# Retention and two expert layers on one core: the second experts' second product by seven sub-products, in passes 2 and 3

## The chip, the cores and the metric

One core of a Trainium2 chip. The metric is the device time of one execution in microseconds, as the median of several runs. TensorE (PE), VectorE (DVE), ScalarE (ACT), GpSimd (POOL) and SyncE (SP, which only issues transfers here) work through queues of their own, each in its order, and wait for one another by semaphores.

## The reference

Three stages, one after the other. `x` has 2304 tokens and 512 features; an expert layer has 8 experts with 1024 hidden features.

```python
scores = scale * np.matmul(q, k.transpose(0, 1, 3, 2))          # 4 batches, 8 heads, 576 positions, 64
attn = np.matmul(scores * Dmat, v)                              # Dmat: decay with distance, causal

for e in range(E):                                              # first experts: each token goes to one
    h = np.maximum(x[expert_idx == e] @ w1[e], 0.0)
    out[expert_idx == e] = gate_w[expert_idx == e, None] * (h @ w2[e])

for e in range(E):                                              # second experts: each token goes to all
    h = np.maximum(x @ w1[e], 0.0)
    out += P[:, e:e + 1] * (h @ w2[e])                          # P: 8 rounds of row and column scaling
```

## The kernel before

Every float32 operand of a large product is split into two terms, a rounded one (`hi`) and the rest (`lo`), and each product is three matmuls: hi x hi, hi x lo, lo x hi. ScalarE makes `hi` by a copy, VectorE or GpSimd `lo` by a subtraction (`lo_of`, L215).

The second experts take nearly all of the time after 378 us. They go over the tokens in 3 passes (`NP`) of 768, in each over the 8 experts, and for each expert over four units of 128 + 128 hidden features. A pass's tokens are two halves of 384 (`GRP`). A unit (`unit`, L1149) holds:

- the first product by Winograd's scheme, seven products in place of eight: `product(j, ...)` is 6 matmuls with 128x128 weights as stationary operand and 384 tokens as moving columns (L1163 to L1165). They add up in two PSUM banks, `xb` and `yb`, so that the bank has to be copied (`keep`, L1144, ScalarE) or summed (`h_sum`, L1132, VectorE) before the next product is added to it;
- the second product of the unit before (`second`, L1086): for each of 6 token tiles 2 x 3 matmuls with hidden features as stationary operand and 512 output features as columns (L1096 to L1098). It adds up over the four units in six banks and is taken out once an expert and tile (`finish`, L1102, L1114 on VectorE), with the weight P; after the last expert rows are scattered to the output (L100).

The order is written out by hand: blocks of 9 matmuls of `second` stand between two products of the first. The weights stream: raw parts of 512 KB arrive in `raw_p` (L211, on SP), and `split_step` (L218) makes slots of a ring of four, some steps ahead; for first weights GpSimd first makes the sums and differences that the scheme needs (L251, L252), for each pass anew. The operands of the next pass are loaded (`xload`), summed (`xsums`, GpSimd) and split (`xsplit`) in the last units of a pass (`renew`). `clock`, `tick` and `arrives` are estimates that decide only where in the order a split is put.

Of the kernel before, what the change touches and what calls it, by code (L numbers as in the profile page):

```python
# [18 lines left out]
# columns of the packed constants (they depend on the shapes alone)  # L19
C_KS, C_ID, C_LT, C_BASE, C_EXP, C_CAP, NCONST = 0, 40, 168, 296, 305, 313, 321  # L20
# Tokens that the units of the first experts take: the first unit has the expert with the most tokens
# once PICK_AT tiles of 128 are routed, the others follow by their numbers of tokens. Where an expert has
# more than its unit takes, all of them go by anyhow() instead.
# batches, positions and features of a head
SHAPE = (4, 576, 64)
CAPS = (384, 352, 328, 320, 304, 296, 288, 280)
PICK_AT = 10
# [8 lines left out]
def kernel(  # L36
# [33 lines left out]
    ring_p = ctx.enter_context(tc.tile_pool(name="ring", bufs=4))  # L70
# [4 lines left out]
    # what the first experts give, [feature, token], the tokens' rows and logits, one expert after the other  # L75
    x2 = dram.tile([DM, 2 * N], F32, name="x2")
    rid = dram.tile([2 * N, 1], I32, name="rid")
    lg2d = dram.tile([2 * N, E], F32, name="lg2d")

# [15 lines left out]
    def scatter(key, dst, idx, src):  # L95
        """Rows of src to distinct rows of dst: no two scatters of one key meet in a row."""
        if scatters.get(key):
            # no two scatters follow each other directly, so that none has to wait for the one before
            nc.gpsimd.memset(gap, 0.0)
# [7 lines left out]
    # ------------------------------------------------------------ constants  # L107
# [9 lines left out]
    # of the units: experts, places in the list, first outputs, tiles of 128, whether any exceeds its unit,  # L117
    # and first outputs whatever exceeds
    tab = const.tile([128, 6, E], I32, name="tab")

    # ------------------------------------------------------------ weight stream
    # Weights arrive as raw parts of 512 KiB and are split into two float32r terms in slots of a
    # ring, four steps to a slot, some slots ahead of the products that take them.
# [57 lines left out]
    for p in range(NP):  # L181
# [9 lines left out]
    # An estimate of when, by the tensor engine's clock, what has been issued so far is there: so that  # L191
    # no engine is made to wait for a load while it has other work.
# [86 lines left out]
    # ------------------------------------------------------------ attention  # L279
    tiles = _tiles()  # L280

    work = ctx.enter_context(tc.tile_pool(name="work", bufs=1))
    # the operands of products whose other operand are weights: tokens, then hidden features
# [9 lines left out]
    with ExitStack() as at:  # L293
# [5 lines left out]
        # decay and mask of [key, query] within a tile, of even and of odd heads  # L299
# [17 lines left out]
        def warm(n):  # L317
            """Products of ones while the first loads are under way: the tensor engine's clock rises with use"""
            p = bank(7)
            for _ in range(n):  # L320
                nc.tensor.matmul(p[:, 0:128], onesb, onesb, start=True, stop=True)
# [27 lines left out]
        def scale(t):  # L349
            """With the decay from the first position: the queries for the state and the keys that enter it"""  # L350
# [9 lines left out]
        def scores(t):  # L360
            """[key, query] of each head, two heads at a time in the halves of the array"""
# [17 lines left out]
        def states(t):  # L379
            """What the state gives to each head, [feature, query]"""  # L380
# [11 lines left out]
        def new_state(t):  # L392
            """The state after the chunk"""
# [16 lines left out]
        def attend(t):  # L410
            """[feature, query] of each head, two heads at a time"""
# [15 lines left out]
        def xout(t):  # L427
            """Rows of x times their gate, which is positive: it goes through the first expert's relu"""
# [9 lines left out]
            if t < B:  # L438
                # the first gathers, of other rows, find all rows written
# [641 lines left out]
    with ExitStack() as m2:  # L1081
# [67 lines left out]
        def unit(u, pre, mids):  # L1149
# [3 lines left out]
            if u["i"] % 2:  # L1153
                pre["w2"] = u["w2"] = take()
# [216 lines left out]
```

## Time and profile before

| | |
|---|---|
| three runs | 1898.59, 1903.05, 1906.12 us; median 1903.05 |
| profiled execution | span 1900.9 us from the first to the last instruction; of its own time only this span is given |
| attention, routing, first experts | 0 to about 378 us |
| second experts, pass 1 | about 378 to 882 us |
| passes 2 and 3 | about 882 to 1893 us, handover between them near 1383 us |
| TensorE busy | 97% of the span; VectorE 56%, ScalarE 41%, GpSimd 38% |

How to read it: TensorE's busy time is the union of matmul times, and a matmul's time holds the filling and emptying of the array, which overlaps its neighbours; what one costs in a row is the distance between two starts. Idle time of an engine has the work behind it that ended the wait.

### The profile page before, as it was taken

The numbers are of one execution on the slowest core, as the hardware profiler recorded it, in microseconds if no ns is written. First come the engines' busy times: TensorE is split into PE (matmuls) and PEld (weight loads), VectorE is DVE, ScalarE is ACT, GpSimd is POOL, SyncE is SP. The second block draws the span as 40 slices with busy tenths as digits, with TensorE's granted clock in tenths as the row PEclk, the third lists the DMA queues.
The fourth block names the chain that finished last, engine by engine and source line by source line (L and its number), as shares of the span: only waits on it lengthen the run. The fifth ranks groups of instructions, "written<-read, shape, count | busy, mean of one in ns | idle before, by whom it ended". The sixth has DMA issues, their size and how long they took to land.

```text
span 1900.9 us, 28236 instructions
## 1 busy us (share of the span) xinstructions
PE 1847.6 (97%) x10499; PEld 1672.2 (88%) x10499; DVE 1055.0 (56%) x2080; ACT 771.8 (41%) x1630; POOL 724.9 (38%) x862
## 2 busy tenths in 40 slices
PE   7788999999999999999999999999999999999998
PEld 6667999998899999998999999999889999999997
DVE  6864447546655554556555545555575545555553
ACT  2243455544434334434343344434443434343432
POOL 4544567632332332426432323233453333333232
PEclk9989999999999999999999999999999999999999
DMA  9855555531212122222222222232232222121210
GB/s 258 255 144 171 191 192 172 182 103 45 78 56 78 58 87 91 77 67 73 83 78 66 68 67 67 67 101 67 67 100 67 67 67 72 62 78 56 78 44 34
DMA packets 132093, 182.23 MB, mean 96 GB/s; under 512 B 19427, under 2 KB 76003, under 8 KB 131944
## 3 DMA queue, kind: packets, MB, share of 16 engines
q1 hardware_dynamic: 127800, 169.66, 28.4%
q0 software_dynamic: 3712, 9.96, 1.6%
q8 instruction: 85, 1.39, 0.3%
q10 hardware_dynamic: 432, 0.69, 0.1%
q14 instruction: 64, 0.52, 0.1%
HBM read 164.40 MB, written 15.89 MB: 95 GB/s over the span
## 4 chain that ended last, share of the span: by engine, by line
PE 84%; DVE 3%; issue 2%; ACT 1%; POOL 0%; DMA 0%; SPq 0%; POOLq 0%; ACTq 0%; DVEq 0%
PE b L1098 13%; PE b L1096 13%; PE b L1097 13%; PE b L1163 12%; PE b L1165 12%; PE b L1164 12%; PE b L665 3%; PE b L666 3%; PE b L667 3%; DVE lo L215 1%; DVE cl L215 0%; PE b L648 0%; DVE c L1132 0%; DMA rid<-lst 0%; POOL out_dram L100 0%
## 5 line engine op out<-in xcount | busy, mean ns | idle before, releaser
L215 POOL TENSOR_TENSOR lo<-raw,hi 128x256 fp32r<-128x256 f32 x320 | 289.3, 914 | 640.4 <-ACT hi L239 636.4
L1163 PE MATMUL b<-ch,hi 128*128 128x384 f32 x1344 | 454.7, 338 | 6.2 <-DVE c L1132 4.7
L1165 PE MATMUL b<-ch,lo 128*128 128x384 f32 x1344 | 452.9, 337 | 0.0
L1164 PE MATMUL b<-cl,hi 128*128 128x384 f32 x1344 | 452.1, 336 | 0.0
L1098 PE MATMUL b<-hi,HL 128*128 128x512 f32 x1152 | 451.1, 392 | 0.0
L1096 PE MATMUL b<-hi,HH 128*128 128x512 f32 x1152 | 450.7, 391 | 0.0
L1097 PE MATMUL b<-lo,HH 128*128 128x512 f32 x1152 | 450.3, 391 | 0.0
L215 DVE TENSOR_TENSOR lo<-raw,hi 128x256 fp32r<-128x256 f32 (+1 forms) x512 | 304.0, 596 | 153.0 <-ACT hi L239 130.9
L1134 ACT ACTIVATE HH<-c 128x384 fp32r<-128x384 f32 x288 | 151.5, 526 | 530.6 <-DVE c L1132 530.6
L1163 PEld LDWEIGHTS b<-ch,hi 128*128 128x128 f32 x1344 | 253.2, 188 | 29.1 <-DVE c L1132 6.0
L1135 DVE SCALAR_TENSOR_TENSOR HL<-c,HH 128x384 fp32r<-128x384 f32 x288 | 169.2, 588 | 189.3 <-ACT HH L1134 189.3
L1164 PEld LDWEIGHTS b<-cl,hi 128*128 128x128 f32 x1344 | 253.4, 189 | 12.4
L1098 PEld LDWEIGHTS b<-hi,HL 128*128 128x128 f32 x1152 | 216.3, 188 | 46.6
L1165 PEld LDWEIGHTS b<-ch,lo 128*128 128x128 f32 x1344 | 253.3, 188 | 0.0
L1096 PEld LDWEIGHTS b<-hi,HH 128*128 128x128 f32 x1152 | 216.8, 188 | 32.2 <-issue 0.5
L1097 PEld LDWEIGHTS b<-lo,HH 128*128 128x128 f32 x1152 | 216.8, 188 | 32.1
L252 POOL TENSOR_TENSOR sums<-raw 128x256 f32<-128x256 f32 x96 | 73.4, 764 | 392.1 <-DVE lo L215 392.1
L1132 DVE TENSOR_TENSOR c<-b,c 128x384 f32<-128x384 f32 x288 | 158.9, 552 | 91.8 <-PE b L1165 91.6
L239 ACT CAST hi<-raw 128x512 fp32r<-128x512 f32 x320 | 196.1, 617 | 8.5 <-ACTq L786 6.0
L1144 ACT COPY c<-b 128x384 f32<-128x384 f32 x288 | 136.4, 474 | 155.4 <-PE b L1165 155.4
L215 DVE TENSOR_TENSOR lo<-sums,hi 128x512 fp32r<-128x512 f32 x192 | 133.7, 698 | 108.3 <-ACT hi L259 108.2
L1140 DVE SCALAR_TENSOR_TENSOR HL<-b,HH 128x384 fp32r<-128x384 f32 x96 | 53.5, 558 | 192.4 <-ACT HH L1139 192.4
(168 smaller groups left out, 2065.9 us busy)
## 6 DMA issues: line engine op xcount, KB each, us to landing
raw<-in_moe_w_dram SPq DMA_DIRECT2D x256, 512.0 KB, 3.7
kT<-in_kT_dram SPq DMA_DIRECT2D x18, 256.0 KB, 5.9
qT<-in_qT_dram SPq DMA_DIRECT2D x18, 256.0 KB, 4.7
v<-in_v_dram SPq DMA_DIRECT2D x18, 256.0 KB, 5.3
xs<-x SPq DMA_DIRECT2D x18, 256.0 KB, 3.9
x<-x SPq DMA_DIRECT2D x12, 384.0 KB, 5.7
k<-in_k_dram SPq DMA_DIRECT2D x16, 256.0 KB, 5.3
qdec<-in_decays_dram SPq DMA_DIRECT2D x4, 256.0 KB, 6.2
```

The costliest lines, as they stand in the source:

```text
L215: eng.tensor_tensor(lo, x, hi.bitcast(F32), ALU.subtract)
L239: nc.scalar.copy(c.hi[:, o:o + 512], x[:, i:i + 512])
L1096: nc.tensor.matmul(y[t], hh[:, s], w.hi[:, f0:f0 + 512], start=first, stop=False)
L1097: nc.tensor.matmul(y[t], hh[:, s], w.lo[:, f0:f0 + 512], start=False, stop=False)
L1098: nc.tensor.matmul(y[t], hl[:, s], w.hi[:, f0:f0 + 512], start=False, stop=end)
L1132: nc.vector.tensor_tensor(c, ps, add, ALU.add)
L1134: nc.scalar.activation(hh, c, AF.Relu)
L1135: nc.vector.scalar_tensor_tensor(hl, c, 0.0, hh.bitcast(F32), ALU.max, ALU.subtract)
L1144: nc.scalar.copy(c, ps)
L1163: nc.tensor.matmul(ps, a, xh[:, r, :], start=first and r == 0, stop=False, skip_group_check=True)
L1164: nc.tensor.matmul(ps, a, xl[:, r, :], start=False, stop=False, skip_group_check=True)
L1165: nc.tensor.matmul(ps, b, xh[:, r, :], start=False, stop=r == 1, skip_group_check=True)
```

## The change

Pass 1 stays as it is but for one thing: each unit also writes the split sums of its first weights (hi and lo, 14 x 128 columns of 128 rows each, 1.84 MB) to a buffer `w1s` in HBM, from the ring slot, on SP. Ring, slots and units are there for pass 1 alone. After its last unit and the drain of that unit's second product, the ring's memory is given to new pools.

Passes 2 and 3 are 16 steps (an expert in a pass each). The first product is the same 7 x 6 matmuls of 384 columns in each of four quarters; its weights come from `w1s` in four groups a quarter, into five buffers. What it gives is kept as relu(h) in float32 in four quadrants (two halves of tokens by two halves of hidden features, each in two parts `kh`). The second product goes by seven sub-products of the quadrants too: VectorE makes four sums of quadrants for each `kh` in place, GpSimd four sums of the second weights' quadrants, ScalarE and VectorE split all seven operands of either kind (14 weight splits of 512 columns and 14 hidden splits of 768 a step). A sub-product of one `kh` and one tile of 128 tokens is a chunk of 6 matmuls with 256 columns. The sub-products add up in six banks of 256 columns; each has its eviction (21 a step) into one half of an accumulator's row, times P. Chunks of a step stand between the first products of the next step, by `GAPS`; after the last step its 42 chunks run alone.

The order of the other engines is no longer written by hand: each piece of work is a `Task` with an engine, a duration and what it waits for; due times are worked back from TensorE's line, and a list scheduler walks simulated time and issues on each engine the ready task that is due first. The operand sums of pass 3 are VectorE tasks now (GpSimd's before). In the rest only comments are gone.

```diff
+    early = ExitStack()
-    ring_p = ctx.enter_context(tc.tile_pool(name="ring", bufs=4))
+    ring_p = early.enter_context(tc.tile_pool(name="ring", bufs=4))
+    w1s = dram.tile([E * 4, 128, 2, 1792], F32, name="w1s")
...
-    for p in range(NP):
+    for p in range(1):
         for e in range(E):
             for j in range(2):
...
         def unit(u, pre, mids):
             w = take()
+            for k, x in enumerate((w.hi, w.lo)):
+                nc.sync.dma_start(out=w1s[4 * u["e"] + u["i"]][:, k], in_=x[:, 0:1792].bitcast(F32))
+            arrives(5.2)
...
-        n_unit = NP * E * 4
+        n_unit = E * 4
...
+    early.close()
+    with ExitStack() as m3:
+        HB = GRP // 128
+        free = {
+            "w1": slots_of("wa", 5, (128, 2, 512), F32R),
+            "w2": list(zip(slots_of("wbh", 4, (128, 2, 256), F32R), slots_of("wbl", 4, (128, 2, 256), F32R))),
+            "h": slots_of("hq", 14, (128, 2, GRP)),
+            "s": list(zip(slots_of("sh", 3, (128, 2, GRP), F32R), slots_of("sl", 3, (128, 2, GRP), F32R))),
...
+        for s in range(first_s, last_s):
+            p, e = divmod(s, E)
+            for i in range(4):
+                kh = i // 2
...
+                    def wload(_, b=b, c0=c0, c1=c1, n=4 * e + i):
+                        nc.sync.dma_start(out=b.tile[:, :, 0:c1 - c0].bitcast(F32), in_=w1s[n][:, :, c0:c1])
+                    wg[gi].load = Task("SP", 4e-3 * (c1 - c0), wload, takes=b)
...
+                product(0, [prev["x"]])
+                made["p1"] = Task("ACT", 0.37, keeper("p1"), [P_[0]], takes=kb["p1"])
+                product(1, [prev["y"]])
+                a0 = put(0, "DVE", 0.47, adder(0, "p1"), [P_[1], made["p1"]], uses=[kb["p1"]])
+                relu[0, i] = Task("ACT", 0.41, relu_in(0), [a0], uses=[hb[0, kh]])
+                product(2, [made["p1"]])
+                made["u2"] = Task("ACT", 0.37, keeper("u2"), [P_[2]], takes=kb["u2"])
+                product(3, [made["u2"]])
+                made["u3"] = Task("ACT", 0.37, keeper("u3"), [P_[3]], takes=kb["u3"])
+                product(4, [made["u3"]])
+                relu[2, i] = put(2, "ACT", 0.39, relu_ps(2), [P_[4]])
+                product(5, [a0])
+                a3 = put(3, "DVE", 0.47, adder(3, "u3"), [P_[5], made["u3"]], uses=[kb["u3"]])
+                relu[3, i] = Task("ACT", 0.41, relu_in(3), [a3], uses=[hb[3, kh]])
+                product(6, [a3])
+                a1 = put(1, "DVE", 0.47, adder(1, "u2"), [P_[6], made["u2"]], uses=[kb["u2"]])
...
+            UB, US = (0.51, 0.60), (0.73, 0.87)
+            for kh in range(2):
+                t3 = Task("POOL", 1.45, sub(T3[kh], B[1, 1], B[0, 1]), [lb[1, 1], lb[0, 1]], takes=T3[kh], uses=[B[1, 1], B[0, 1]], wide=True)
+                s0 = split("w2", 0, kh, B[0, 0], [lb[0, 0]], UB)
+                t5 = Task("POOL", 1.45, sub(B[0, 1], B[0, 1], B[0, 0]), [t3, lb[0, 0]], uses=[B[0, 1], B[0, 0]], wide=True)
...
+                z4 = Task("DVE", 0.87, add(z4b, Q[1], Q[3]), done[1] + done[3], takes=z4b, uses=[Q[1], Q[3]], wide=True)
+                s0 = split("s", 0, kh, Q[0], done[0], US)
+                z2 = Task("DVE", 0.87, sub(Q[1], Q[0], Q[1]), [z4, *done[0]], uses=[Q[0], Q[1]], wide=True)
+                z0 = Task("DVE", 0.87, sub(Q[0], z4b, Q[0]), [z2, s0], uses=[Q[0], z4b], wide=True)
...
+            def chunk2(j, kh, t, sops=sops, bops=bops, ps2=ps2):
...
+                    for r in range(2):
+                        st = kh == 0 and j in (0, 1, 5) and r == 0
+                        nc.tensor.matmul(ps, hh[:, r, c], wh[:, r], start=st, stop=False, skip_group_check=True)
+                        nc.tensor.matmul(ps, hh[:, r, c], wl[:, r], start=False, stop=False, skip_group_check=True)
+                        nc.tensor.matmul(ps, hl[:, r, c], wh[:, r], start=False, stop=kh == 1 and r == 1, skip_group_check=True)
...
+            for j in range(7):
+                for kh in range(2):
+                    for t in range(HB):
+                        so, bo = sops[j, kh], bops[j, kh]
+                        dep = [so[1], so[2], bo[1], bo[2]]
+                        if kh == 0:
+                            back = {0: 4, 1: 6, 2: 0, 3: 2, 4: 3, 5: 1, 6: 5}[j]
+                            dep.append(ev.get((back, t)) if j > 1 else last_ev.get((back, t)) if s > first_s else None)
+                        c = pe(0.714, chunk2(j, kh, t), dep, uses=[so[0], bo[0]])
+                for t in range(HB):
+                    eng, us, fn = evict(j, t)
...
+        GAPS = (1, 1, 2, 2, 1, 3, 0.5)
+        for s in range(first_s, last_s + 1):
+            b = [g2[s - 1, j, kh, t] for j in range(7) for kh in range(2) for t in range(HB)] if s > first_s else []
+            owed = 0
+            if s < last_s:
+                for i in range(4):
+                    for j in range(7):
+                        line.append(g1[s, i, j])
+                        owed += GAPS[j]
+                        while owed >= 1:
+                            owed -= 1
+                            if b:
+                                line.append(b.pop(0))
+            line += b
```

## Rows read from the trace of the kernel before

**Rows 1.** The page: span, then busy us, share and instructions of an engine.

```profile
span 1900.9 us, 28236 instructions
...
PE 1847.6 (97%) x10499; PEld 1672.2 (88%) x10499; DVE 1055.0 (56%) x2080; ACT 771.8 (41%) x1630; POOL 724.9 (38%) x862
```

**Rows 2.** Stretches: length; busy of PE, PEld, DVE, ACT, POOL; clock; DMA share; GB/s.

```profile
175.00:378.00 203.00, 198.06 (x1400) 191.14 (x1401) 106.34 (x194) 104.19 (x216) 123.42 (x129) 0.98 0.57 182
...
902.00:1362.00 460.00, 460.00 (x2315) 415.79 (x2314) 244.55 (x432) 183.75 (x388) 150.56 (x186) 1.00 0.23 74
1362.00:1402.00 40.00, 37.34 (x178) 33.02 (x177) 28.38 (x37) 18.60 (x35) 26.98 (x25) 0.96 0.22 75
```

**Rows 3.** Groups, whole span: count; busy us, mean ns; idle before, releaser.

```profile
L1163 PE MATMUL b<-ch,hi 128*128 128x384 f32 x1344 | 454.7, 338 | 6.2 <-DVE c L1132 4.7 <-ACT c L1144 0.9
...
L1098 PE MATMUL b<-hi,HL 128*128 128x512 f32 x1152 | 451.1, 392 | 0.0
```

**Rows 4.** TensorE's timeline in a unit of pass 2: start, duration, line, shapes.

```profile
1008.08 0.39 PE L1096 MATMUL b<-hi,HH 128*128 128x512 f32 x1
...
1010.14 0.34 PE L1163 MATMUL b<-ch,hi 128*128 128x384 f32 x1
...
1012.23 0.39 PE L1096 MATMUL b<-hi,HH 128*128 128x512 f32 x1
```

**Rows 5.** TensorE's timeline, the last first experts: first and last of 46.

```profile
371.76 0.29 PE L667 MATMUL b<-HH,lo 128*128 128x280 f32 x1
...
377.52 0.29 PE L667 MATMUL b<-HH,lo 128*128 128x280 f32 x1
```

**Rows 6.** TensorE's timeline in the attention, eight matmuls in one line.

```profile
46.26 1.06 PE L388 MATMUL b<-qs,st 128*128 128x128 f32 x8
```

**Rows 7.** TensorE's timeline at both handovers; brackets: idle before, releaser.

```profile
884.78 0.45 PE L1163 MATMUL b<-ch,hi 128*128 128x384 f32 x1 [2.34 <-DVE c L1132]
...
893.88 0.45 PE L1163 MATMUL b<-ch,hi 128*128 128x384 f32 x1 [0.56 <-ACT c L1144]
...
1385.70 0.69 PE L1163 MATMUL b<-ch,hi 128*128 128x384 f32 x1 [2.33 <-DVE c L1132]
1386.18 0.52 PE L1164 MATMUL b<-cl,hi 128*128 128x384 f32 x1
...
1388.42 0.52 PE L1165 MATMUL b<-ch,lo 128*128 128x384 f32 x1
```

**Rows 8.** The last matmul of a product, and ScalarE's copy of its bank.

```profile
1003.76 0.34 PE L1165 MATMUL b<-ch,lo 128*128 128x384 f32 x1
...
1004.19 0.48 ACT L1144 COPY c<-b 128x384 f32<-128x384 f32 x1 [1.82 <-PE b L1165]
```

**Rows 9.** VectorE's timeline, and below it GpSimd's, in the same unit.

```profile
1008.33 1.16 DVE L215 TENSOR_TENSOR lo<-raw,hi 128x512 fp32r<-128x512 f32 x1
...
1013.13 0.69 DVE L215 TENSOR_TENSOR lo<-sums,hi 128x512 fp32r<-128x512 f32 x1
...
1008.20 0.74 POOL L251 TENSOR_TENSOR sums<-raw,sums 128x256 f32<-128x256 f32 x1
```

**Rows 10.** Groups with shapes kept apart, whole span: count; busy us, mean ns.

```profile
L1132 DVE TENSOR_TENSOR c<-b,c 128x384 f32<-128x384 f32 x288 | 158.9, 552 | 91.8 <-PE b L1165 91.6
...
L1134 ACT ACTIVATE HH<-c 128x384 fp32r<-128x384 f32 x288 | 151.5, 526 | 530.6 <-DVE c L1132 530.6
...
L1114 DVE SCALAR_TENSOR_TENSOR a<-b,P,a 128x512 f32<-128x512 f32 x126 | 86.9, 741 | 2.8 <-PE b L1098 2.8
...
L259 ACT CAST hi<-sums 128x512 fp32r<-128x512 f32 x192 | 118.4, 617 | 6.0 <-POOL sums L251 6.0
...
L358 POOL TENSOR_TENSOR qs<-qT,qdec 128x512 f32<-128x512 f32 x14 | 17.7, 1263 | 1.3 <-PE b L400 0.9 <-DMA qdec<-in_decays_dram 0.4
...
L980 ACT CAST ch<-x 128x768 fp32r<-128x768 f32 x18 | 14.9, 828 | 1.4 <-POOL x L961 1.4
```

**Rows 11.** DMA issues: queue, count, KB each, median us from issue to landing.

```profile
raw<-in_moe_w_dram SPq DMA_DIRECT2D x256, 512.0 KB, 3.7
```

317 lines of the change are left out of this document (316 added, 1 removed).

## Prediction

> **What bounds the kernel now.** I read the page's first part, then the table by stretch, then the groups by line, then TensorE's own timeline. The page says that TensorE is busy for 97% of the span [rows 1]; a share alone doesn't tell whether it works at its peak, so the stretches come next. In the 460 us from 902 to 1362, which lie in passes 2 and 3, TensorE is busy for 460.00 us at granted clock 1.00, VectorE for 245, ScalarE for 184, GpSimd for 151, and the DMA engines for 23% [rows 2]. Nothing else comes near: in these passes the time is the number of matmuls times their spacing. Only around 1362 to 1402, where a pass hands over to the next, does TensorE lose 2.7 us [rows 2].
>
> The mean durations in the groups (338 and 392 ns [rows 3]) are no price, since matmuls overlap. The spacing is: nine matmuls of 512 columns start between 1008.08 and 1010.14, so 2.06 / 9 = 0.2289 us each; twelve of 384 columns take the next 2.09 us, 0.174 each [rows 4]. A unit has 42 of 384 (first product) and 36 of 512 (second product): 7.3 + 8.2 = 15.5 us. An expert has four units in a pass, 62.2 us.
>
> **What the change takes off TensorE.** The first product stays: 168 x 0.174 = 29.2 us for an expert and pass. The second goes from 144 matmuls of 512 columns (144 x 0.2289 = 33.0 us) to 7 sub-products x 2 halves x 3 tiles x 6 = 252 of 256 columns. The columns fall to 7/8, but the number of matmuls rises by three quarters, so all hangs on the spacing at 256 columns, which the trace doesn't have. The nearest row is 280 columns: 45 steps from 371.76 to 377.52 us are 0.128 each [rows 5]. Over columns at 2.4 GHz (0.213, 0.160, 0.117 us) the three rows have 15, 14 and 11 ns more. 256 columns are 0.107 us at that clock; with 11 to 15 ns it is 0.118 to 0.122, and I take 0.119. That is 252 x 0.119 = 30.0 us, 2.97 us less for an expert and pass, and for 16 of them **-47.5 us**. Bounds: -51.5 at 0.118, and -11 us (252 x 0.128 = 32.3 us) if 256 columns are no quicker than 280.
>
> The Trainium skill ("TensorE: Matmul & The Clock Gate", Back-to-back issue gap) gives columns over 2.4 GHz plus 2.5 ns: 215.8 and 109.2 ns, by which the change would take off 57 us; the trace's 0.229 at 512 disagrees, so the rows decide.
>
> **What it adds.**
> The kernel before keeps a block of the second product between any two of the first; the list in the new order keeps one to three chunks there, taken from the expert before. The first expert of pass 2 has no expert before, since the pass-1 loop ends with its own drain. There products 3, 4 and 6 of each quarter stand right behind the copy or sum of the bank that they add to. Such a copy starts 0.26 us after TensorE's next slot (matmul at 1003.76, slot at 1003.93, copy at 1004.19), takes 0.48 [rows 8], so it ends 0.74 us after that slot; the matmul that waited for it then starts, 0.05 later by the estimate from the same pair of engines, and takes 0.45 us where others take 0.34 (893.88 [rows 7]): 0.9 us in all. Twelve of them are **+10.8 us** (8 to 18: the upper end where each also stands behind one 0.62 us cast).
>
> The last expert's second product (30 us) now runs alone at the end, behind its own splits. Of VectorE's work for it, 14 weight residuals at 0.69, 22 operations of 768 columns at 1.04 (0.69 x 768/512) and 21 evictions at 0.45 (between a half of 0.74 and all of it), 42 us [rows 9, 10], about 8 can be done ahead with three split buffers and four weight pairs: 34 against 30, **+4 us** (0 to 12).
>
> In the steady part VectorE has for each expert and pass these 42 us and 12 sums at 0.55, in all 49 us of 59.2 us; ScalarE 12 x 0.47 + 16 x 0.53 + 14 x 0.62 + 14 x 0.83 = 34 us [rows 8, 10]. GpSimd's eight weight sums at about 1.26 us [rows 10] are 10 us, and they can delay VectorE: a 512-column residual alone took 0.69 us, but 1.16 when it started at 1008.33 while a GpSimd sum ran from 1008.20 to 1008.94; from 1008.94 on it is 0.55 to its end [rows 9]. So VectorE waited, it did not share. Full serial cost is 49 + 10 = 59 us, just the period. Orders on all engines are fixed, so a late eviction or copy stops TensorE: queued behind a waiting VectorE sum are evictions of the second product, and the next sub-product of the same bank waits for those. Bounds: 0 (as now) to one late 0.56 us [rows 7] in each quarter, 36 us over all; I take one for each expert and pass, 16 x 0.6 = **+9.6 us**.
>
> The Trainium skill ("SBUF — State Buffer", SBUF: two separate sides) calls that port pair an exclusive lock, held for a whole instruction; the 1.16 us row agrees, and it speaks against this change, which moves VectorE towards its limit.
>
> Handover of pass 2 to 3: now a sum waits 2.33 us at 1385.70 and the nine matmuls after it run 0.32 apart, that is at the lower of the two clocks (1.2 GHz), for another 1.3 us [rows 7]. The new order has the operand sums on VectorE, nine more operations of 1.04 us in about 30 us that have 0 to 10 free for each 59: I keep the same 4 us, **0** (-4 to +6). Handover of pass 1 to 2: the last unit's 2.34 us wait stays, since that code stays; the 0.56 behind it goes, because the drain of 36 matmuls (8.2 us) now stands there: **-1**. The same 8.2 us cover the first loads of pass 2 (512 KB land in 3.7 us [rows 11]) as long as ring slots of earlier units are free; **+1**, 5 without that cover.
>
> Removed at no gain: splits, sums and ring of the first weights in passes 2 and 3, since TensorE doesn't wait for them now [rows 2]. What stands in their place is loads: 4 x 1.84 MB of split weights and 2.1 MB of second weights in 59 us, 160 GB/s; in pass 1 the writes add 32 x 1.84 = 58.7 MB in 32 x 15.5 = 496 us to the 74 GB/s that a pass moves now, 192 GB/s. The stretch 175 to 378 moved 182 GB/s with the DMA engines 57% busy [rows 2], so both fit. The writes stand on SP behind the split of the slot just taken, with the raw loads queued behind them; those run some units ahead: **+1** (0 to 5).
>
> Sum: 1900.9 - 47.5 + 10.8 + 4 + 9.6 + 0 - 1 + 1 + 1 = **1878.8 us** of span. The median of the runs shown is 1903.05, 2.1 above the profiled span; I add that: **1880.9 us**, 1.2% less.
>
> **Rivals.**
> *The weight load becomes the bound.* A multiply of 256 columns is 107 ns; full 128x128 loads with only 128 columns behind them run at (1.06 - 0.29) / 7 = 0.110 us a pair [rows 5, 6] (0.29 for the time of the last one itself, as that of the nearest row), though their columns are half that. So the load needs almost what the multiply does, and if the two don't overlap well, 256 columns stay at the 0.128 of 280. Each ns costs 252 x 16 = 4.0 us: at 0.128, 1917 us, **slower**. It decides from 0.127. Against it: 0.110 is below 0.119, and at 280 columns nothing of it is seen. Chance 9%. The Trainium skill (same page, LDWEIGHTS) prices a load of 128 columns at 107 ns, and the 0.110 row agrees.
>
> *VectorE becomes the pace.* With stops of 2.2 us for each expert and pass it is 1880.9 - 9.6 + 35.2 = 1906 us, no change (12%); from 2.6 us it is slower, 1919 at 3 (6%). For it: the 49 to 59 us against 59. Against: the 59 needs every GpSimd sum to fall on a waiting VectorE operation, and the new order puts two chunks (2 x 6 x 0.119 = 1.4 us) and most often a first product (6 x 0.174 = 1.0 us) between an eviction and the matmul that needs its bank.
>
> *Nothing stops.* No late evictions, handovers covered, a drain in time: 1880.9 - 9.6 - 4 - 4 = 1863 us, faster (20%).
>
> *The reload doesn't do what it says*: weights come late from HBM. One 3.7 us landing exposed for each expert and pass is +59, 1940 us (2%). Against: five buffers, each used some 4 us of 18.
>
> **How the numbers follow.** Forecast 51%, of which 5% lie above the line of no change. What a measurement can tell from no change is 0.5%, 9.5 us: faster is below 1893.5, slower above 1912.5. Faster 0.46 + 0.20 = 0.66; same 0.05 + 0.12 = 0.17; slower 0.09 + 0.06 + 0.02 = 0.17. The range goes from 1855 (nothing stops, 4 less at 0.118 and 4 less at the handover) to 1913, which leaves out the load, slow VectorE and reload cases.
>
> **What would show it.** Spacing of 256-column matmuls in the last 30 us, where nothing else runs: 0.119; 0.127 or more is the first rival. TensorE's idle time by what it waited for: about 11 us in the first 40 us of pass 2, 4 at the end, 10 spread over the rest, on VectorE and ScalarE. VectorE near 50 us of each 59. No wait for loads. Pass 1 unchanged to within 2 us. The forecast falls with the spacing, or with idle time in the middle of a pass above 1.3 us for each expert.

## The result, and the profile after

The changed kernel takes 1880.87 us (median of 4 runs, 1880.26 to 1886.72); the kernel before took 1902.31 us on the same chip (median of 4, 1898.59 to 1906.12). The ratio is 0.9901 with an interval of 0.9879 to 0.9924: 1.0% faster. The profiled execution took 1880.59 us, its span is 1878.8 us. The forecast was 1880.9 us, with a span of 1878.8. That the two agree to the last digit is luck: the mechanism and the largest term were right, but three of the smaller terms were off by 10, 10 and 4 us, one of them because its step was wrong, and they cancel.

The page of the kernel after, against [rows 1] (span; busy us, share and instructions of each engine; then two groups of matmuls with count, busy us, mean ns, and idle time before them by releaser):

```profile
span 1878.8 us, 32676 instructions
...
PE 1803.9 (96%) x12227; PEld 1720.0 (92%) x12227; DVE 1233.2 (66%) x2239; ACT 892.2 (47%) x1718; POOL 575.1 (31%) x599
...
L1566 PE MATMUL b<-wbh,sh 128*128 128x256 f32 x1344 | 379.7, 282 | 2.1 <-DVE ya L1585 2.1
...
L1385 PE MATMUL b<-ch,wa 128*128 128x384 f32 x896 | 304.8, 340 | 17.6 <-ACT kp L1391 7.4
```

The work moved as the change says: GpSimd is busy for 150 us less, VectorE for 178 us more. The last group has what is new: 17.6 us of idle time before the matmuls of the first product, 7.4 of it for one copy, `kp`.

The table by stretch of the kernel after, to be read against [rows 2] (length; busy us of PE, PEld, DVE, ACT, POOL, with instructions; granted clock; DMA share; GB/s):

```profile
376.00:860.00 484.00, 483.74 (x2489) 437.72 (x2488) 267.74 (x508) 197.91 (x417) 158.47 (x191) 1.00 0.54 192
892.00:901.00 9.00, 1.56 (x9) 1.25 (x8) 0.52 (x1) 0.48 (x1) 1.89 (x3) 0.71 1.00 333
901.00:943.00 42.00, 32.98 (x154) 28.78 (x154) 11.23 (x18) 16.87 (x33) 10.26 (x8) 0.90 0.64 197
943.00:1350.00 407.00, 407.00 (x2887) 406.89 (x2886) 308.67 (x465) 223.12 (x399) 69.73 (x53) 1.00 0.54 166
1400.00:1780.00 380.00, 380.00 (x2699) 380.00 (x2698) 285.57 (x430) 207.07 (x371) 77.95 (x65) 1.00 0.54 164
```

Inside a pass TensorE never stops (407.00 of 407 and 380.00 of 380). Most of what is lost lies at one place, 892 to 943, the start of pass 2, in whose first 9 us TensorE worked for 1.56. The traffic is what was forecast: 192 GB/s in pass 1 (192), 166 and 164 in passes 2 and 3 (160).

The spacing, which carries the forecast, in the timeline of TensorE of the kernel after, against [rows 4] (start, duration; first a chunk and a half in pass 2, nine matmuls of 256 columns from 1007.46 up to the 384-column matmul at 1008.54; then the first and the last of the 30 matmuls that end the kernel):

```profile
1007.46 0.28 PE L1566 MATMUL b<-wbh,sh 128*128 128x256 f32 x1
...
1008.54 0.34 PE L1385 MATMUL b<-ch,wa 128*128 128x384 f32 x1
...
1864.48 0.28 PE L1566 MATMUL b<-wbh,sh 128*128 128x256 f32 x1
...
1867.96 0.28 PE L1568 MATMUL b<-wbh,sl 128*128 128x256 f32 x1
```

From 1007.46 to 1008.54 are nine steps, 0.120 each; from 1864.48 to 1867.96 are 29, also 0.120. Over the long stretches 0.1195 fits best. The forecast took 0.119.

**Where the time went.** For the sums below, the "excess" of a stretch is TensorE's time from matmul start to matmul start beyond the plain spacing (0.1195 us at 256 columns, 0.1736 at 384, 0.2285 at 512). From the first matmul of pass 1's units (377.64 before, 377.89 after) to the last matmul of all (1892.61, 1867.96) the kernel takes 1514.97 us before and 1490.07 after: 24.9 less. By terms:

| term | forecast | measured |
|---|---|---|
| 256 columns for 512: 16 x (144 x 0.2285 - 252 x 0.1195) | -47.5 | -44.6 |
| stops of pass 2's first expert behind bank copies and sums | +10.8 | +12.2 |
| handover 1 to 2: the new wait for `kp` 7.6, low clock after it 3.5 | +1 | +11.1 |
| handover 1 to 2: stalls of pass 1's last unit | -1 | -4.6 |
| steady part, 950 to 1350 and 1400 to 1780 (before -0.4, after -1.1) | +9.6 | -0.7 |
| handover 2 to 3 (4.95 before, 1.98 after) | 0 | -3.0 |
| last second product (-0.1 before, 4.5 after) | +4 | +4.6 |
| pass 1, writes (1.93 before, 1.80 after) | +1 | -0.1 |
| sum to the last matmul | -22.1 | -25.1 |
| after the last matmul (8.29 before, 10.84 after) | 0 | +2.55 |
| ahead of pass 1 | 0 | +0.25 |

The terms give -22.3 and the spans differ by -22.1. The stretch 860 to 950, which holds the handover and all twelve stops, has 4.6 us of excess before and 23.3 after.

### The profile page after: what moved, and what is told of

Same layout as the page of the kernel before. It is cut to its first block, busy times and chain, and to the rows that moved or that the text cites. A ratio compares the mean times of both kernels' runs of the same rounds, so it can differ in the third digit from the quotient of the medians.

```text
span 1878.8 us, 32676 instructions
## 1 busy us (share of the span) xinstructions
PE 1803.9 (96%) x12227; PEld 1720.0 (92%) x12227; DVE 1233.2 (66%) x2239; ACT 892.2 (47%) x1718; POOL 575.1 (31%) x599
## 4 chain that ended last, share of the span: by engine, by line
PE 84%; DVE 3%; ACT 1%; issue 1%; DMA 1%; POOL 0%; SPq 0%; ACTq 0%; DVEq 0%; POOLq 0%
PE b L1568 8%; PE b L1567 8%; PE b L1566 8%; PE b L1385 8%; PE b L1386 8%; PE b L1387 8%; PE b L1100 5%; PE b L1102 5%; PE b L1101 5%; PE b L1170 4%; PE b L1172 4%; PE b L1171 4%; PE b L669 3%; PE b L671 3%; PE b L670 3%
## 5 line engine op out<-in xcount | busy, mean ns | idle before, releaser
L1566 PE MATMUL b<-wbh,sh 128*128 128x256 f32 x1344 | 379.7, 282 | 2.1 <-DVE ya L1585 2.1
L1568 PE MATMUL b<-wbh,sl 128*128 128x256 f32 x1344 | 380.3, 283 | 0.5 <-DVE sl L219 0.4
L1567 PE MATMUL b<-wbl,sh 128*128 128x256 f32 x1344 | 380.6, 283 | 0.0
L1385 PE MATMUL b<-ch,wa 128*128 128x384 f32 x896 | 304.8, 340 | 17.6 <-ACT kp L1391 7.4
L1386 PE MATMUL b<-cl,wa 128*128 128x384 f32 x896 | 302.3, 337 | 0.0
L1387 PE MATMUL b<-ch,wa 128*128 128x384 f32 x896 | 300.8, 336 | 0.0
L1568 PEld LDWEIGHTS b<-wbh,sl 128*128 128x128 f32 x1344 | 257.5, 192 | 0.9 <-DVE sl L219 0.9
L1385 PEld LDWEIGHTS b<-ch,wa 128*128 128x128 f32 x896 | 170.6, 190 | 22.7 <-ACT kp L1391 7.8
L1387 PEld LDWEIGHTS b<-ch,wa 128*128 128x128 f32 x896 | 168.9, 189 | 0.0
L1170 PE MATMUL b<-ch,hi 128*128 128x384 f32 x448 | 151.6, 338 | 0.3
L1172 PE MATMUL b<-ch,lo 128*128 128x384 f32 x448 | 150.5, 336 | 0.0
L1171 PE MATMUL b<-cl,hi 128*128 128x384 f32 x448 | 150.3, 336 | 0.0
```

What stands on the lines that cost most here:

```text
L1170: nc.tensor.matmul(ps, a, xh[:, r, :], start=first and r == 0, stop=False, skip_group_check=True)
L1171: nc.tensor.matmul(ps, a, xl[:, r, :], start=False, stop=False, skip_group_check=True)
L1172: nc.tensor.matmul(ps, b, xh[:, r, :], start=False, stop=r == 1, skip_group_check=True)
L1385: nc.tensor.matmul(ps, a, xh[:, r, :], start=first, stop=False, skip_group_check=True)
L1386: nc.tensor.matmul(ps, a, xl_[:, r, :], start=False, stop=False, skip_group_check=True)
L1387: nc.tensor.matmul(ps, b, xh[:, r, :], start=False, stop=r == 1, skip_group_check=True)
```

## The experiments

Each is an edit of the changed kernel. The time before pass 1's units, which no edit touches, differs between the runs (its end lies at 372.81 to 381.19 us), so where a few us matter I count from the first matmul of these units to the last matmul of all: 1490.07 us in the kernel after. Times are medians of four runs unless it says one run; ratios are to the kernel before, run beside them.

**What holds the first copy of pass 2?** The chain of waits of the kernel after, from the last matmul of pass 1 on (start, duration, what), and under it ScalarE's timeline (in brackets the idle time before and what ended it):

```profile
890.76 0.24 PE b L1102
...
891.02 0.76 DVE a L1118
...
891.88 0.96 POOL out_dram L104
...
893.15 6.72 DMA out_dram<-a,idc
...
899.97 0.49 ACT kp L1391
...
900.50 0.69 PE b L1385
```
```profile
899.97 0.48 ACT L1391 COPY kp<-b 128x384 f32<-128x384 f32 x1 [15.23 <-DMA out_dram<-a,idc]
```

The copy of the first bank waits for the transfer of pass 1's last scatter. It is not its data that it needs. The scatter reads an accumulator `a` of pass 1, and the theory is that the memory of `kp`, allocated anew for passes 2 and 3, lies where that accumulator lay. The first edit lets `kp`, `ku`, `kv` take other memory, by allocating them ahead of the split operands:

```diff
+            "p1": slots_of("kp", 1, (128, GRP)),
+            "u2": slots_of("ku", 1, (128, GRP)),
+            "u3": slots_of("kv", 1, (128, GRP)),
             "s": list(zip(slots_of("sh", 3, ...
-            "p1": ...   (the three lines moved up)
```

> The changed kernel with one edit: the three buffers for the bank copies (kp, ku, kv) are laid ahead of the split buffers, so that the first of them no longer lies where pass 1's accumulators were. Theory A (the first copy of pass 2 waits until the last scatter of pass 1 has left the accumulator under it): ScalarE's copy starts some 0.3 us after the first product, the 7.4 us wait of the third product at 900.5 shrinks to about 0.6, TensorE's clock doesn't fall, so the 24 or so matmuls at 0.32 us go back to 0.174: 6.8 + 3.5 = about 10 us less, a span near 1868 us. Rival B (the copy waits for the first weights of pass 2 or for the ring as a whole): the wait stays within 1 us of 7.4, span 1878 to 1880.

1868.15 us (1864.02 to 1870.52), ratio 0.9832 [0.9807, 0.9856]. ScalarE's timeline and TensorE's waits from 885 to 945 us (total us, times, longest):

```profile
890.51 0.48 ACT L1391 COPY kp<-b 128x384 f32<-128x384 f32 x1 [7.38 <-issue]
```
```profile
PE b L1385 <- DVE hq L1397: 2.9, 4, 0.7
PE b L1385 <- ACT ku L1391: 2.4, 4, 0.6
PE b L1385 <- ACT kv L1391: 2.4, 4, 0.6
PE b L1385 <- DMA wa<-w1s: 2.0, 1, 2.0
```

The copy now runs at 890.51 and no longer waits; the 7.4 us wait for `kp` is gone from the list. So it was the memory. Not all comes back: a wait of 2.0 us for the weights, `wa`, shows further on, and the expectation that the clock would not fall failed, since the lower clock follows behind that wait (stretch of this run, under the columns of the table above):

```profile
906.00:912.00 6.00, 5.43 (x18) 4.92 (x16) 1.03 (x1) 0.97 (x2) 4.09 (x4) 0.50 0.80 266
```

That costs some 2.5 us. The excess from 860 to 950 falls from 23.3 to 16.0, and the time between the two matmuls by 8.9 us; of the rest 1.4 us lies in the last second product, where the low clock described below was shorter.

The twelve stops stand there as forecast: three kinds of four, 0.6 to 0.7 us each. In the kernel after one of them is longer, 2.0 us; ScalarE makes that copy behind two casts. Its waits in the same stretch, the two that differ from the list above:

```profile
PE b L1385 <- ACT kp L1391: 7.4, 1, 7.4
PE b L1385 <- ACT ku L1391: 3.8, 4, 2.0
```

The second edit changes the first expert's order so that products 3, 4 and 6 no longer stand right behind the copy or sum of their bank:

```diff
-                    for j in range(7):
+                    for j in (0, 1, 2, 5, 3, 4, 6) if s == first_s else range(7):
```

> The changed kernel with one edit: in the first step of pass 2, where no second product stands between the first products, TensorE takes the seven products of a quarter in the order 0, 1, 2, 5, 3, 4, 6 instead of 0 to 6. Product 5 starts the other bank and so can cover the copy behind product 2, and product 4 the sum that product 6 needs; only the copy behind product 3 stays uncovered. Theory A (what TensorE loses there are three copies or sums of a bank a quarter, 0.9 us each): eight of twelve stops go, some 7 us less, span near 1872 us, with the 7.4 us wait of the first quarter still there. Rival B (the stops are VectorE and ScalarE being behind with the splits of that step, or weights arriving late): the same time is lost at other products, span within 2 us of 1879.

1868.35 us (1863.57 to 1869.16), ratio 0.9834 [0.981, 0.9858]. TensorE's waits from 885 to 945 us:

```profile
PE b L1385 <- ACT kp L1391: 8.0, 1, 8.0
PE b L1385 <- ACT kv L1391: 2.3, 4, 0.6
PE b L1385 <- ACT ku L1391: 0.9, 1, 0.9
```

The copy of `kp` holds it up as before; of the twelve stops the four of `kv` stay and one of `ku`, so seven go where eight were expected. The excess from 860 to 950 is 14.6 instead of 23.3. This is 8.7 us; seven stops at the forecast's 0.9 and 1.1 off the longest one are 7.4, and the lower clock behind the wait for `kp` holds some 1.6 us less, though the wait is 0.6 longer. The profiled span, 1865.9, is 6.1 us below the expected 1872: 2.5 us of that lies again in the last second product and 1.6 ahead of pass 1, neither of which the edit touches.

**How far is VectorE from being the pace?** The forecast allowed 9.6 us for late evictions; none is seen. Either there is much room, or little. Doubling each of GpSimd's weight sums (a second operation on the result, times one) lengthens what GpSimd holds of the port that it shares with VectorE; `sub` and `add` call it:

```diff
+            def again(eng, o, y, z, op):
+                eng.tensor_tensor(o, y, z, op)
+                if eng is nc.gpsimd:
+                    w = o.rearrange("p k (a c) -> p (k a) c", c=128)
+                    eng.tensor_tensor(w, w, ones.unsqueeze(1).to_broadcast([128, 4, 128]), ALU.mult)
```

> The changed kernel with one addition: after each of GpSimd's eight weight sums of a step (passes 2 and 3) GpSimd multiplies the result by ones, another operation of 512 columns with two inputs, so that it works twice as long; the order on every engine stays. Theory A (TensorE is free of VectorE's delays, since VectorE was busy for only 45 of 59 us and two chunks stand behind most evictions): VectorE's busy time goes up by at most 10 us a step, to 55, and TensorE's idle time in the middle of a pass stays under 0.5 us a step: span under 1887 us. Rival B (the forecast's: one late eviction of 0.6 us a step, and more with each collision): 0.6 us or more a step, 16 steps, span 1889 us or more; at a full 1.3 us stop for each added operation far over 1900.

Two more make VectorE's own sum larger: the residuals of the second weights computed twice, and all residuals of the second product computed twice.

```diff
-                    lo_of(nc.vector, o.tile[1], src.tile, o.tile[0])
+                    for _ in range(2 if kind == "w2" else 1):
+                        lo_of(nc.vector, o.tile[1], src.tile, o.tile[0])
```

> The changed kernel with one addition: in passes 2 and 3 VectorE makes the residual of each of the 14 weight splits of a step twice, one right after the other, 8.4 us more a step (14 x 0.6); the order on every engine stays. VectorE goes from 45 to about 54 of 59 us. Theory A (VectorE paces only when its own sum reaches the step, and what doubled GpSimd work cost was its late start of single sums, not its total): at most 0.6 us a step, span under 1889 us. Rival B (the order has so little room that each late operation stops TensorE): 1.5 to 3 us a step as with doubled GpSimd work, whose VectorE was at 48.5 us: span 1903 to 1927 us.

```diff
-                    lo_of(nc.vector, o.tile[1], src.tile, o.tile[0])
+                    for _ in range(2):
+                        lo_of(nc.vector, o.tile[1], src.tile, o.tile[0])
```

> The same for all 28 residuals of a step: 8.4 + 14 x 0.87 = 20.6 us more, VectorE would need 66 us a step. Both theories: it paces. If its sum alone decides, the step is 66 us, 7 more than now, and the span 1879 + 16 x 7 = 1990 us; if waits add to it, more. It gives the point from which VectorE decides.

They took 1923.04, 1952.88 and 2166.33 us (one run each). The stretch 943 to 1350 of each, in this order, under the columns of the table above:

```profile
943.00:1350.00 407.00, 397.02 (x2792) 394.39 (x2791) 334.94 (x448) 212.20 (x384) 153.31 (x100) 1.00 0.53 160
```
```profile
943.00:1350.00 407.00, 391.45 (x2697) 387.87 (x2698) 356.93 (x522) 204.15 (x372) 66.54 (x48) 0.98 0.51 156
```
```profile
943.00:1350.00 407.00, 340.73 (x2228) 329.75 (x2229) 364.89 (x503) 169.26 (x308) 56.96 (x40) 0.96 0.42 129
```

And TensorE's waits in it (total us, times, longest), of the first and of the last:

```profile
PE b L1385 <- DVE hq L1397: 9.5, 8, 1.5
```
```profile
PE b L1385 <- DVE hq L1397: 44.9, 33, 4.1
PE b L1385 <- ACT ku L1391: 14.2, 10, 1.9
PE b L1567 <- DVE ya L1586: 3.5, 4, 0.9
```

An expert and pass is 168 x 0.1736 + 252 x 0.1195 = 59.3 us of plain spacing. The excess of the stretch (-0.5, 12.7, 25.9 and 91.4 us) says how many of these it holds: (407 - excess) / 59.3 = 6.87, 6.65, 6.43 and 5.32. For one expert and pass that makes:

| kernel | VectorE busy | GpSimd busy | excess |
|---|---|---|---|
| after | 44.9 | 10.2 | -0.1 |
| sums on GpSimd twice | 50.4 | 23.1 | 1.9 |
| weight residuals twice | 55.5 | 10.3 | 4.0 |
| all residuals twice | 68.6 | 10.7 | 17.2 |

This is the rival of VectorE's pace, and the runs give its curve. At 44.9 us of 59.3 nothing is lost; at 50.4, with 9 us to spare by its own sum, each expert already loses 1.9 us; at 68.6, 9.3 above the period, it loses 17.2, so 8 us more than the sum. That the gaps would swallow an addition fell with the first of the three, and the numbers for the other two were missed, the last by 175 us of span against VectorE's sum alone. In the first two runs what TensorE waits for is nearly always the sum `hq`. In the first it is one such wait of 1.4 to 1.5 us for each expert and pass, and each time VectorE comes to the sum straight from a weight residual, as here ahead of the matmul at 1020.49, which waited 1.45 us:

```profile
1019.28 0.68 DVE L219 TENSOR_TENSOR wbl<-sums,wbh 128x512 fp32r<-128x512 f32 x1
1019.89 0.55 DVE L1397 TENSOR_TENSOR hq<-b,kv 128x384 f32<-128x384 f32 x1
```

So a sum is late because it stands in a fixed order behind something longer, and TensorE has no slack to win it back. In the third run copies, evictions and residuals are late as well. The first of the three runs shows the price of the shared port too: 12.9 us more of GpSimd lengthened VectorE's busy time by 5.5 us though its instructions are the same (67 in an expert and pass in both). The added time lies in the operations whose two inputs are both in SBUF (a weight residual 711 ns in the kernel after, 950 here); an eviction (478, 476) and a bank sum (555, 550), which read a bank, stay as they were. No engine waited for GpSimd's results in that stretch.

The Trainium skill ("SBUF — State Buffer", SBUF: two separate sides) says that GpSimd and VectorE take that port in turns, one waiting until the other's instruction ends. The 5.5 us are in line with that; how long each wait lasts they don't show.

**How near is the weight load?** A load that needed more than 0.119 us was the rival that ended slower. To see its floor, two of the three matmuls of a triple take 128 columns instead of 256, with the same weight loads (the low terms of the other columns are left out of the result):

```diff
-   nc.tensor.matmul(ps, hh[:, r, c], wl[:, r], ...)
-   nc.tensor.matmul(ps, hl[:, r, c], wh[:, r], ...)
+   nc.tensor.matmul(ps[:, 0:128], hh[:, r, c], wl[:, r, 0:128], ...)
+   nc.tensor.matmul(ps[:, 0:128], hl[:, r, c], wh[:, r, 0:128], ...)
```

> The changed kernel, but in the second product of passes 2 and 3 the two matmuls of each three that carry a low term take only the first 128 of their 256 columns; the low terms of the other columns are left out of the result. Theory A (a matmul's spacing is its columns over the clock and some 12 ns, down to 256 columns and on): 128 columns follow at 0.066 us, a step's second product takes 84 x (0.1195 + 2 x 0.066) = 21 us, the step 50 us, and the span falls by 130 us or more unless VectorE's 45 us a step come into the way. Theory B (the weight load is just under the multiply at 256 columns, by the 0.110 us of the 128-column pairs in the attention): 128 columns follow at 0.110, a step's second product takes 28.5 us instead of 30.1, and the span falls by about 25 us, to 1854. By B the load was not the bound at 256 but lies 9 ns under it.

1876.17 us (one run). The weight loads (PEld) and the matmuls (PE) of one chunk, from the timeline:

```profile
1100.95 0.19 PEld L1568 LDWEIGHTS b<-wbh,sl 128*128 128x128 f32 x1
...
1101.98 0.19 PEld L1568 LDWEIGHTS b<-wbh,sl 128*128 128x128 f32 x1
```
```profile
1100.84 0.28 PE L1566 MATMUL b<-wbh,sh 128*128 128x256 f32 x1
...
1102.83 0.39 PE L1385 MATMUL b<-ch,wa 128*128 128x384 f32 x1
1103.06 0.34 PE L1386 MATMUL b<-cl,wa 128*128 128x384 f32 x1
```

Nine loads take 1.03 us, 0.114 each. The eighteen matmuls take 1.99 us instead of 18 x 0.1195 = 2.15, and the next one is 0.23 instead of 0.17 before its successor, so the chunk is some 0.10 shorter though a third of its columns are gone. From the first matmul of pass 2's second expert to the first of pass 3's last, fourteen experts, it takes 813.3 us instead of 830.8, 1.25 each. By its columns each would have been some 9 us shorter (128 columns at about 0.066, an estimate from columns over 2.4 GHz and the some 12 ns that the wider rows have on top: 168 x 0.053). So a load with its matmul has a floor of 0.114, and 256 columns stand only 5 to 6 ns above it. That the load sets this floor, and not something else that each pair of load and matmul costs, was not tested. The rival was wrong at this width, by a narrow margin, and with a load for each matmul anything narrower has little left to gain: 4032 x 0.0055 = 22 us in the whole kernel.

The Trainium skill ("TensorE: Matmul & The Clock Gate", LDWEIGHTS) gives a load's time as its columns over 1.2, in ns, by which 128 columns would take 107 ns (an estimate from that formula); in this run they come 114 ns apart.

**Both gains together.** The two edits of the handover, and a due time for the last scatters, which had none, so that the evictions ahead of them would be placed earlier:

```diff
+        for t in given.values():
+            t.due = clock_
         for t in reversed(order):
```

> The two edits of the earlier runs together (bank copies' buffers first; order 0, 1, 2, 5, 3, 4, 6 in the first step of pass 2), and the last row scatters are given a due time, so that the evictions before them aren't put off behind everything else. Theory A (the costs were separate): the excess of TensorE's spacing in the first step falls from 23 us to four copies of 0.75 us and some 2 us of weights that come late, about 5 us; the last scatter starts 1 to 2 us sooner after the last matmul (now 4.0 us). Span 1878.8 - 18 - 1.5 = about 1859 us. Rival B (with the stops gone, the first weights from HBM become late): the wait moves to the loads, span 1863 to 1868.

1861.84 us (1859.05 to 1863.45), ratio 0.9797 [0.9775, 0.9818]. TensorE's waits from 885 to 945, the first of its final scatters in GpSimd's timeline, and the same one of the kernel after:

```profile
PE b L1385 <- DMA wa<-w1s: 3.9, 2, 2.2
PE b L1385 <- ACT kv L1391: 2.4, 4, 0.6
```
```profile
1843.95 0.98 POOL L104 DMA_INDIRECT out_dram<-ya,idc  x1 [22.11 <-DVE ya L1585]
```
```profile
1865.65 0.99 POOL L104 DMA_INDIRECT out_dram<-ya,idc  x1 [23.52 <-DVE ya L1585]
```

From the first matmul of pass 1's units to the last it takes 1473.45 us, 16.6 less than after: 15.0 at the first handover (23.3 to 8.3) and 2.7 at the second handover and at the end, with 1.2 lost again in small parts over the passes. The due time did nothing: the first scatter starts 2.31 us ahead of the last matmul (1846.26 here, 1867.96 after) in both kernels. And part of the gain went into a new wait, 3.9 us for the first weights.

Those weights are issued late. The theory of the last run is that they wait for memory of pass 1 as `kp` did, so in the combined version the accumulators and the three copies were allocated ahead of everything else:

```diff
+        acc = slots_of("ya", 3 * HB, (128, DM))
         free = {
+            "p1": ..., "u2": ..., "u3": ...   (moved ahead of the other kinds)
```

> The combined version with the memory laid out once more: the accumulators of passes 2 and 3, which are first written a step later, take the first place of the ring's memory, then the bank copies, then the weight buffers. Theory A (SP's loads were late in the first step because the third weight buffer lay on the ring slot that the drain reads, so that SP stood from 866 to 891 us with all second weights queued behind): the loads are issued before the drain ends, the two waits for first weights of 1.6 and 2.2 us in the first step go, span 1857.3 - 4 = about 1853 us. Rival B (the first step asks more of HBM than it gives, 7.3 MB and second weights in 40 us): the waits move by the time of some loads but stay, span 1856 to 1859.

1858.11 us (1854.01 to 1859.36), ratio 0.9778 [0.974, 0.9816]. The median is 3.7 us below that of the run before, but the intervals of the ratios overlap, so a gain is not shown. The profiled executions, the fastest of the run before and the slowest of this one, take 1473.45 and 1473.89 us from first to last matmul, with 8.3 and 9.9 us of excess at the first handover. TensorE's waits from 885 to 945, SP's queue and its longest wait, and two stretches:

```profile
PE b L1385 <- DMA wa<-w1s: 3.7, 1, 3.7
PE b L1385 <- ACT kv L1391: 2.3, 4, 0.6
```
```profile
877.53 8.69 SPq L1367 DMA_DIRECT2D wa<-w1s  x5
886.27 4.71 SPq L1494 DMA_DIRECT2D raw<-in_moe_w_dram  x6
```
```profile
SPq L1367 <- PE b L1172: 24.4, 1, 24.4
```
```profile
870.00:878.00 8.00, 8.00 (x42) 7.18 (x41) 4.47 (x6) 3.68 (x6) 5.31 (x3) 1.00 0.00 0
892.00:901.00 9.00, 5.27 (x28) 4.98 (x27) 5.23 (x8) 5.33 (x10) 3.27 (x2) 0.87 1.07 386
```

The two waits became one of nearly the same sum. In the kernel after SP's issue of `wa` waits there for the last second product of pass 1 (L1102; 33.8 us in all, 23.3 the longest); now it waits 24.4 us for a matmul of the last first product (L1172) instead. So the wait for memory of pass 1 moved from one reader to another and did not go; which buffer it is was not found, and stays open. The stretches speak for the rival too: nothing is moved from 870 to 878, while SP stands, and from 892 to 901, where TensorE waits, the DMA engines are busy throughout at 386 GB/s. Which of the two decides, the late start or the full engines, was not tried.

## Why the forecast was right, and where it was not

**The spacing** (forecast -47.5, measured -44.6). 0.119 was worked out from the three widths in [rows 4, 5], and 0.1195 was measured. Half a nanosecond is 2 us here; the 512-column spacing, 0.2285 and not 0.2289, is the rest. The bound of 0.128 (no gain from 280 to 256) did not come about.

**The stops of the first expert** (+10.8, +12.2). The step was right in kind, place, count and price: waits of 0.57 to 0.72 us behind the banks' copies and sums, 0.84 to 0.99 of excess with the slow start behind each. One wait was 2.0, and that is the difference. The product order showed that seven of them come from the order; the five that stayed are those that it left uncovered, and one more.

**Handover 1 to 2** (+1, +11.1). This is the step that failed. I asked whether the drain covers the loads of pass 2, and looked at ring slots only; I didn't ask who still reads the memory in which the new buffers stand. The changed kernel's scatter of the last accumulator takes 0.96 us on GpSimd and 6.72 in transfer, and `kp` lay under it. In the same handover the forecast left a wait of 2.34 us [rows 7] in place because "that code stays". It went, and the small ones around it (4.6 us for the 1 forecast). What VectorE no longer does there, splitting the next pass's first weights, is the likely reason; that is argued and was not tried.

**Late evictions** (+9.6, -0.7). The mis-sized term. VectorE's sum was taken as 49 us for an expert and pass, and the durations of its operations do add up to 48.6; but one starts before the one ahead of it has ended (1019.89 and 1019.96 in the two rows above), so VectorE is busy for 44.9. One late stop of 0.6 for each expert and pass was taken from this nearness to the period, not from a row, and from 943 to 1350 TensorE has no wait at all; the -0.7 is spacing a little under the 0.1195 and 0.1736 taken. The experiments show that the mechanism is real and begins at most 5.5 us of busy time higher, so the term was the right one to have, at a wrong place on its curve.

**Handover 2 to 3** (0, -3.0). The wait of 2.33 us and the slow matmuls behind it [rows 7] became two of 0.7 and 0.5 us. I kept 4 us for more operations on VectorE; probably the covering second product, 30 us of TensorE's work, counted for more, which was not tried.

**The end** (+4, +4.6, and +2.55 after the last matmul). The last second product waits for VectorE as forecast, once for 2.10 us instead of in small pieces, and the matmuls after it run at the lower clock for 3 us. Not foreseen: six scatters, 1.27 us apart on GpSimd, start 2.31 us ahead of the last matmul where they started 5.05 ahead before (1887.56 against 1892.61), so they end 2.6 us later.

So +10.1 at the first handover, +2.9 in the spacing, +2.55 at the tail, +1.4 in the stops and small ones stand against -10.3 in the steady part, -3.6 and -3.0 at the handovers and -1.1 in pass 1. Of the rivals, "nothing stops" (1863 us) came near in the steady part and was wrong at both ends; a kernel with its handover mended, at 1861.84, is about there.

## What to carry to other kernels

When a change allocates buffers anew for a later stage, ask of each who read that memory last: a scatter or store can hold it for its whole transfer, here 6.7 us, although no data passes between the two. Where a bank is reused right after its copy, put an independent product between the two; one line of order was worth 8.7 us here, the shorter low clock included. An engine in a fixed order becomes late well before its own sum fills the period (at 50 us of 59 here), so a forecast of "it still fits" needs a price as well.

## What the runs showed of the chip

- Weight loads of 128 columns come 0.114 us apart when two of three matmuls behind them have 128 columns; matmuls of 256 columns are 0.1195 apart. The difference, 5 to 6 ns, is all that narrower matmuls with a load each could gain.
- Waits of 2 to 3 us are not followed by the same clock each time. The wait of 2.10 us ahead of 1844.93 in the kernel after is followed by matmuls 0.42 us long (0.28 otherwise) until 1848, at the lower clock; the same wait of 2.10 us ahead of 1824.64 in the kernel with both gains by none:

```profile
1844.93 0.55 PE L1566 MATMUL b<-wbh,sh 128*128 128x256 f32 x1 [2.10 <-DVE ya L1585]
```
```profile
1824.64 0.36 PE L1566 MATMUL b<-wbh,sh 128*128 128x256 f32 x1 [2.10 <-DVE ya L1585]
```

  In the kernel with narrow columns a wait of 2.64 us ahead of 1828.1 was followed by the lower clock for all of the last 38 us, as its table by stretch shows (PEclk 0.50 is 1.2 of 2.4 GHz), though TensorE was busy for 37.88 of them:

```profile
1828.00:1866.00 38.00, 37.88 (x178) 37.91 (x178) 21.62 (x37) 8.93 (x13) 4.16 (x8) 0.50 0.06 22
```

  Of the 17.5 us that its fourteen experts gained, 13.4 are lost again from the first matmul of the last expert on, and 3.9 ahead of the fourteen, so that 0.2 is left from first to last matmul. What keeps the clock down there was not tried.
